# One buffer for x1*x3, four for chunks of x and f_logit, and no gate on the recurrence, in a gated recurrence followed by a Hyena convolution

## The chip, the cores and the metric

The kernel runs on one core of a Trainium2 chip. The metric is the device time of one execution in microseconds (us), the median of several executions. Profiles come from one further execution under the hardware profiler. The engines are TensorE (PE; its weight loads are shown apart as PEld), VectorE (DVE), ScalarE (ACT), GpSimd (POOL) and SyncE (SP, which here issues all DMAs). Each engine takes its instructions strictly in the order in which the program lists them for it; engines wait for each other through semaphores.

## The reference

```python
# x, f_logit: [4, 6272, 256], lower_bound: [256]
f = lower_bound + (1 - lower_bound) * sigmoid(f_logit)
h[t] = f[t] * h[t-1] + (1 - f[t]) * x[t]            # over t, h[-1] = 0
proj = h @ w_proj                                    # [4, 6272, 768]
x1, x2, x3 = split(proj, 3)                          # 256 each
x2_conv = irfft(rfft(x2, axis=1) * rfft(filter_fft, axis=0), axis=1)   # circular, length 6272
out = (x1 * x2_conv * x3) @ w_out
```

## The kernel before

The length S = 6272 is taken as 128 x 49, and the Fourier transform as two matmul stages over these factors. Before the batches, `prepare` makes the transform matrices and the spectrum of the filter, which goes to DRAM in 16 pieces `H[u]`. The first batch's recurrence runs beside it. Each batch then passes through these parts:

- `hgrn(b)`, the recurrence, in 13 chunks of 512 time steps (the last has 128). A chunk of `f_logit` and one of `x` are loaded into the buffers `FL` and `XT` (L279-282; `NX` of each, so chunk c + NX waits for the transposes of chunk c). ACT takes the sigmoid (L283), POOL multiplies with it (L285), PE transposes both (`turn`, L294; the tasks are `sT` and `uT`), ACT turns the sigmoid into f (`fTs`, L306), and DVE scans along time (L311) into the tile `HA`, whose halves hold h for the two halves of the channels. POOL copies h once more into a contiguous region of `HA` (L262, "copy E"), which phase_p reads with a stride and which also holds, as `A`, the first-stage transform (`E`) of the batch before until its unit has read it. From the second batch on, the transposes of f_logit's chunk c also wait (`late`, L288) for the inverse matmuls of unit `AFTER[c]` of the batch before.
- `phase_p(b)` (L589) projects h to x2, `phase_f1(b)` (L604) does the first transform stage, `mini(b)` the zero frequencies.
- `units(b)`: 16 units of 8 channel pairs. Each loads its piece of H into one of the `Hu` buffers (L641), does the second transform stage on PE (L648), a small copy into `PP` on POOL (L651), the product with H on DVE (L658, two of them), the inverse stage on PE (L668) and a copy of its result into `Th`.
- `gate(b, u)`, called at the end of unit u: for the row chunks in `GATES[u]`, PE computes x1 and x3 (L340, four tasks of two matmuls for one chunk), ACT copies them to `x1s` and `x3s` (L350; two buffers each), and POOL multiplies them into the tile z (L354, two per chunk). A gate of unit u > 0 waits for the second transform stage of unit u (`("F", u)`); that of unit 0 waits for the last transposes of the same batch's recurrence (`"qT"`). The gate matmuls read h in `HA`, chunks c - 1 and c, and so the next batch's scan may overwrite these chunks only behind them.
- `phase_o(b)`: the last inverse stage (L694), the product with z on DVE (L701, into `ys`), the projection by w_out (L711), a copy and the store. phase_p of the next batch waits for the stores that go out of the space behind x2.

The order of each engine's instructions is made when the program is built. Every operation is handed to `Plan.op` with a guessed cost on each engine that may do it, what it reads and what it writes; `Plan.emit` is a list scheduler. It goes through the engines, takes for each the operations that can start first by its guesses, among these the one with the longest remaining path (`level`), and issues the earliest. Costs in the code are, for n columns, 0.12 + 2.2 n/1000 us for z, 0.1 + 0.535 us per 128 time steps for the product of x and the sigmoid, 0.07 + 2.25 n/1000 for a scan. DMAs are guessed at 300 KB per us, one behind the other. All batches behind the first prepare stage are one plan, so operations of neighbouring batches may overlap as far as the listed dependences allow. PSUM's eight banks are handed out by the same planner.

z has a buffer `z0` for even batches and `z1` for odd ones, 25 KB per partition each; `z0` lies in the pool that lives from the start, `z1` in `cv`, which begins behind the first recurrence.

Of the kernel before, what the change touches and what calls it, by code (L numbers as in the profile page):

```python
# [11 lines left out]
F16 = mybir.dt.float16  # L12
# [12 lines left out]
Q = 49  # L25
TB = 98
CH = 512
NX = 2
NCHK = 13

AFTER = (2, 5, 7, 10, 12, 15)

GATES = [[0, 1, 2], [3], [4], [5], [6], [7], [8], [9], [10], [11], [12]] + [[]] * 5
XR = 10
NEP = 128
UE = 8
NU = NEP // UE
# [151 lines left out]
def kernel(  # L189
# [17 lines left out]
    konst = ctx.enter_context(tc.tile_pool(name="konst", bufs=1))  # L207
# [16 lines left out]
    HA = konst.tile([128, 2 * S + EW], F16, name="HA")  # L224
    A = HA[:, S:S + EW].rearrange("m (e r k) -> m e r k", r=2, k=64)
    HB = (0, S + EW)

    z0 = konst.tile([128, 2, Q, 128], F16, name="z0")
    XT = konst.tile([128, NX, 4, D], F32, name="XT")
    FL = konst.tile([128, NX, 4, D], F32, name="FL")  # L230
    fTs = konst.tile([128, 2, CH], F32, name="fTs")
    x1s = konst.tile([128, 2, CH], F32, name="x1s")
# [31 lines left out]
    def either(n, runs=1.0):  # L264

        return {"ACT": 0.15 + runs * n / 1200.0, "DVE": 0.15 + runs * n / 960.0}
# [4 lines left out]
    def hgrn(b):  # L271
        for c in range(NCHK):
            t0 = c * CH
            nb = min(CH, S - t0) // 128
            n = nb * 128
            k = count["x"] % NX
            count["x"] += 1
# [9 lines left out]

            late = [("U", AFTER[min(c, len(AFTER) - 1)])] if b else []  # L288
            for kh in range(2):
# [34 lines left out]


    def gate(b, u):
        z = zt[b % 2]
        for c in GATES[u]:
            m0 = c * XR
            nm = min(XR, 128 - m0)  # L330
            hn = [("hn", kh, i) for kh in range(2) for i in range(max(c - 1, 0), c + 1)]
            t0, n = m0 * Q, nm * Q
            for jb in range(2):
                x13 = []
                for i in range(2):
                    js = slice(i * 256 + jb * 128, i * 256 + jb * 128 + 128)

                    def mm(e, p, js=js, t0=t0, n=n):
                        for kh in range(2):
                            nc.tensor.matmul(PS[:, p, 0:n], W13[:, kh, js],  # L340
                                             HA[:, HB[kh] + t0:HB[kh] + t0 + n],
                                             start=(kh == 0), stop=(kh == 1))
                    x13.append(op({"PE": 2 * n / 2400.0}, mm,
                                  r=hn + ["W13", ("F", u) if u else "qT"], w=["qX"], take=1))
                j = count["s"] % 2
                count["s"] += 1
                xs = [t[:, j, 0:n] for t in (x1s, x3s)]
                for i in range(2):
                    op({"ACT": 0.15 + n / 1200.0}, lambda e, p, xs=xs[i], n=n, i=i:
                       nc.scalar.activation(  # L350
                           xs, PS[:, p, 0:n], AF.Copy, scale=1.0 if i else ZS),
                       w=[("x1s", j, i)], src=x13[i])
                op({"POOL": 0.12 + 2.2 * n / 1000}, lambda e, xs=xs,
                   zz=z[:, jb, :, m0:m0 + nm]: nc.gpsimd.tensor_tensor(  # L354
                       zz, xs[0].rearrange("p (m r) -> p r m", r=Q),
                       xs[1].rearrange("p (m r) -> p r m", r=Q), op=AOP.mult),
                   r=[("x1s", j, 0), ("x1s", j, 1)], w=[("z", b % 2, jb, c)])


    def prepare(tmp):  # L360
# [275 lines left out]
    def units(b):  # L636
        for u in range(NU):
            es = slice(u * UE, (u + 1) * UE)
            k = u % 2
            h = (b * NU + u) % 3  # L640
            op({"SP": 0.5}, lambda e, h=h, u=u: nc.sync.dma_start(Hu[:TB, h], H[u][:]),  # L641
               r=[("H", u, i) for i in range(3)], w=[("Hu", h)], kb=400)

            def mm(e, xb, es=es):
                for r in range(2):
                    for e2 in range(2):
                        rows = slice(64 * e2, 64 * e2 + 64)
                        nc.tensor.matmul(PS[:, xb + e2, :], FT[rows, r, :], A[rows, es, r, :],  # L648
                                         start=(r == 0), stop=(r == 1))
            f2 = op({"PE": 0.5}, mm, r=[("E", u)], w=[("F", u)], take=2)  # L650
            op({"POOL": 0.35}, lambda e, k=k, es=es: nc.gpsimd.tensor_copy(  # L651
                PP[:TB, k, :, :, :, 0], zm[:TB, :, :, es]), r=["zm"],
               w=[("Pz", k, 0), ("Pz", k, 1)])
            for o in range(2):
                def prod(e, xb, o=o, k=k, h=h):
                    px = PS[:TB, xb + o, :].rearrange("p (i k) -> p i k", k=64)[:, :, 1:64]
                    hh = Hu[:TB, h, :, o].rearrange("p a (i k) -> p a i k", k=64)
                    nc.vector.tensor_tensor(  # L658
                        PP[:TB, k, o, :, :, 1:64],
                        px.unsqueeze(1).broadcast_to([TB, 2, UE, 63]), hh[:, :, :, 1:64],  # L660
                        op=AOP.mult)
                op({"DVE": 1.2}, prod, r=[("Hu", h)], w=[("P", k, o)], src=f2)

            def inv(e, ib, k=k):
                for o in range(2):
                    for pr in range(UE // 2):
                        for n, v in enumerate((VA, VB)):
                            nc.tensor.matmul(PS[:, ib + o, pr * TB:(pr + 1) * TB],  # L668
                                             PP[:TB, k, o, n, 2 * pr:2 * pr + 2, :], v[:TB],
                                             start=(n == 0), stop=(n == 1))  # L670
            i2 = op({"PE": 0.96}, inv, r=[("P", k, 0), ("P", k, 1), ("Pz", k, 0), ("Pz", k, 1)],
                    w=[("U", u)], take=2)
            op(either(784), lambda e, ib, u=u: copy(
                e, Th[:, :, :, u * 4:(u + 1) * 4],
                PS[:, ib:ib + 2, 0:392].rearrange("p a (g c) -> p c a g", g=4)),
               r=[("x2", g) for g in range(13)], w=["Th", ("Th", u)], src=i2)
            gate(b, u)


    def phase_o(b):  # L680
        zr = zt[b % 2][:].rearrange("p k r m -> p k (r m)")
        tf = Th[:].rearrange("p c a g -> p (c a g)")
        for g, r0 in enumerate(range(0, Q, 4)):
            rn = min(4, Q - r0)

            def inv(e, cb, r0=r0, rn=rn):
                for i in range(rn):
# [13 lines left out]
               nc.vector.tensor_tensor(  # L701
                   y, PS[:, cb:cb + 2, 0:rn * 128], zr[:, :, r0 * 128:(r0 + rn) * 128],
                   op=AOP.mult),
               r=[("z", b % 2, jb, c) for jb in range(2) for c in range(NCHK)],
               w=[("y", yk)], src=i1)

            def proj(e, ob, y=y, rn=rn):
# [6 lines left out]
            k = count["o"] % 2  # L714
# [4 lines left out]
               r=[("x2o", i) for i in range(14)] if k else [], w=[("osb", k)], src=po)  # L719
# [3 lines left out]
               r=[("osb", k)] + ([("x2o", i) for i in range(14)] if k else []), kb=128 * rn)  # L723

    def gaps(p):

        a = X2[:, p * PW:NEP * PW].rearrange("m (i c) -> m i c", c=PW)
        nc.gpsimd.memset(a[:, :, Q:64], 0.0)
        nc.gpsimd.memset(X2[:, NEP * PW:NEP * PW + 16], 0.0)

    zt = [z0, None]
    with tc.manual_schedule():
        with tc.tile_pool(name="tmp", bufs=1) as tmp:
            prepare(tmp)
            hgrn(0)
            plan.emit()
        cv = ctx.enter_context(tc.tile_pool(name="cv", bufs=1))
        zt[1] = cv.tile([128, 2, Q, 128], F16, name="z1")
        X2 = cv.tile([128, NEP * TB + 2048], F16, name="X2")
        Th = X2[:, 0:NEP * TB].rearrange("p (c a g) -> p c a g", a=2, g=64)  # L740

        PP = cv.tile([128, 2, 2, 2, UE, 64], F16, name="PP")
        Hu = cv.tile([128, 3, 2, 2, UE * 64], F16, name="Hu")

        ys = cv.tile([128, 2, 2, 512], F32R, name="ys")
        osb = [cv.tile([128, 4, 256], F32, name="osb0"),
               X2[:, NEP * TB:NEP * TB + 2048].bitcast(F32).rearrange("p (r e) -> p r e", e=256)]
        zm = cv.tile([128, 2, 2, NEP], F16, name="zm")
        gaps(0)
        phase_p(0)  # L750
        phase_f1(0)
        mini(0)
        for b in range(B):
            units(b)
            phase_o(b)
            if b + 1 < B:
                hgrn(b + 1)
                phase_p(b + 1)
                phase_f1(b + 1)
                mini(b + 1)  # L760
        plan.emit()
# [30 lines left out]
```

## Time and profile before

| | us |
|---|---|
| median of 3 runs | 607.95 (606.51 to 609.89) |
| the profiled execution | 613.48 |
| its span, first to last instruction | 611.7 |
| mean granted TensorE clock | 0.917 |

| part | first to last instruction of the line, us |
|---|---|
| scans of the four batches (L311) | 20.2-100.3, 150.2-237.2, 290.0-372.8, 420.4-505.2 |
| phase_p (L589) | 102.7-113.9, 237.7-248.6, 373.8-384.6, 505.5-516.4 |
| second transform stage of the units (L648) | 125.6-183.9, 260.2-312.4, 396.3-452.4, 528.1-570.0 |
| z (L354) | 102.4-190.7, 237.7-321.0, 373.6-458.5, 505.7-577.1 |
| projection in phase_o (L711) | 193.5-234.0, 322.3-362.6, 461.8-502.0, 578.6-604.6 |

A busy time is the time in which an engine worked on an instruction; the share is of the span or of the stretch. A row of the table by stretches gives the stretch, its length, the busy time of each engine with the number of instructions in brackets, the clock granted to TensorE (1.00 is full), the mean share of the 16 DMA engines and what they moved in GB/s. For a single line the same row holds that line's instructions only. A row of a timeline gives start, duration, engine, line, operation, the tiles written and read, the shape and the count; an idle time of the engine before it stands in brackets, with the instruction that ended it. `SPq` is SP's sequencer, whose rows are the issues of DMAs. A row of the waits gives who waited for whom, the total in us, how often, and the longest.

### The profile page before, as it was taken

How to read it: one execution, taken by the hardware profiler on the slowest of the kernel's cores; microseconds unless marked ns; L12 is line 12 of the kernel's file. 1: busy time of each engine (PE TensorE's matmuls, PEld its weight loads, DVE VectorE, ACT ScalarE, POOL GpSimd, SP SyncE). 2: the span in 40 equal slices, each digit the busy share in tenths (PEclk: the TensorE clock that was granted, in tenths of full speed). 3: DMA queues.
4: the chain of work that ended last, by engine and by line, in shares of the span. 5: the costliest groups of instructions: out<-in, count | busy, mean ns of one | idle time of the engine just before them, and what ended most of it. 6: DMA issues, size and time to landing. Idle time of an engine off the chain costs nothing. (4 is left out here: it accounts for less than half of the span.)

```text
span 611.7 us, 12552 instructions
## 1 busy us (share of the span) xinstructions
PE 505.6 (83%) x4821; PEld 377.6 (62%) x4821; DVE 470.2 (77%) x450; ACT 409.6 (67%) x568; POOL 396.0 (65%) x362
## 2 busy tenths in 40 slices
PE   1679977979889888979897859979887969799793
PEld 1668755846457777836466848736466858455483
DVE  8966863899958676989859756899868857989661
ACT  4787774957666577948675656958675759668443
POOL 4455556647998558649896557557995653669700
PEclk9987996979989898979989988989989989989886
DMA  9975888115847897025848984027658960135055
GB/s 313 337 251 193 288 287 259 50 55 177 225 122 230 291 349 244 1 80 158 251 147 283 318 315 139 1 88 226 204 155 266 359 245 11 28 130 168 21 207 215
DMA packets 73038, 117.57 MB, mean 192 GB/s; under 512 B 4366, under 2 KB 55634, under 8 KB 72978
## 3 DMA queue, kind: packets, MB, share of 16 engines
q1 hardware_dynamic: 72978, 116.77, 57.5%
q8 instruction: 38, 0.62, 0.4%
q14 instruction: 22, 0.18, 0.1%
HBM read 84.54 MB, written 32.11 MB: 191 GB/s over the span
## 5 line engine op out<-in xcount | busy, mean ns | idle before, releaser
L354 POOL TENSOR_TENSOR z<-x1s,x3s 128x490 f16<-128x490 f32 (+1 forms) x104 | 200.1, 1938 | 61.7 <-ACT x3s L350 58.8
L658 DVE TENSOR_TENSOR PP<-PS,Hu 98x1008 f16<-98x1008 f32 x128 | 146.3, 1199 | 26.1 <-PE PS L648 7.9
L311 DVE TENSOR_TENSOR_SCAN HA<-fTs,HA,PS 128x512 f16<-128x512 f32 (+1 forms) x96 | 114.7, 1206 | 47.6 <-PE PS L294 38.2
L285 POOL TENSOR_TENSOR XT<-XT,FL 128x1024 f32<-128x1024 f32 (+1 forms) x52 | 118.0, 2271 | 42.7 <-DMA XT<-in_x_dram 22.5
L340 PE MATMUL PS<-HA,W 128*128 128x490 f16 (+1 forms) x416 | 111.3, 388 | 4.1 <-ACT x1s L350 3.3
L252 ACT CAST X<-PS 128x784 f16<-128x784 f32 (+2 forms) x82 | 82.4, 1013 | 32.4 <-PE PS L668 27.3
L294 PE MATMUL PS<-iden,XT 128*128 128x128 f32 x392 | 70.8, 306 | 35.5 <-POOL XT L285 31.5
L262 POOL COPY HA<-HA 128x512 f16<-128x512 f16 (+3 forms) x100 | 59.0, 598 | 61.6 <-DVE HA L311 59.1
L306 ACT ACTIVATE fTs<-PS,nomc 128x512 f32<-128x512 f32 (+1 forms) x104 | 68.7, 664 | 42.2 <-PE PS L294 36.2
L350 ACT ACTIVATE x1s<-PS 128x490 f32<-128x490 f32 (+1 forms) x104 | 60.4, 581 | 43.3 <-PE PS L340 22.1
L294 PE MATMUL PS<-iden,FL 128*128 128x128 f32 x392 | 67.6, 297 | 20.9 <-ACT FL L283 18.6
L294 PEld LDWEIGHTS PS<-iden,XT 128*128 128x128 f32 x392 | 49.2, 155 | 51.1 <-POOL XT L285 36.5
L668 PEld LDWEIGHTS <-PP 98*128 98x128 f16 x1024 | 57.0, 105 | 31.7 <-POOL PP L651 19.1
L701 DVE TENSOR_TENSOR ys<-PS,z 128x1024 fp32r<-128x1024 f32 (+1 forms) x52 | 59.3, 1154 | 19.1 <-PE PS L694 13.8
L668 PE MATMUL PS<-VA,PP 98*128 98x98 f16 x512 | 58.3, 219 | 16.8 <-POOL PP L651 16.0
L340 PEld LDWEIGHTS <-W 128*128 128x128 f16 x416 | 37.3, 102 | 54.1 <-issue 35.1
L711 PE MATMUL PS<-Wo,ys 128*128 128x256 f32 x392 | 63.5, 308 | 5.9 <-DVE ys L701 3.8
L283 ACT ACTIVATE FL<-FL 128x1024 f32<-128x1024 f32 (+1 forms) x52 | 52.4, 1010 | 23.0 <-DMA FL<-in_f_logit_dram 23.0
L294 PEld LDWEIGHTS PS<-iden,FL 128*128 128x128 f32 x392 | 50.3, 153 | 27.8 <-issue 15.5
L350 ACT ACTIVATE x3s<-PS 128x490 f32<-128x490 f32 (+1 forms) x104 | 59.6, 573 | 5.3 <-PE PS L340 5.0
L257 DVE CAST X<-PS 128x1024 f16<-128x1024 f32 (+2 forms) x34 | 45.7, 1369 | 19.4 <-PE PS L589 9.7
L711 PEld LDWEIGHTS PS<-Wo,ys 128*128 128x128 f32 x392 | 53.7, 204 | 9.8 <-issue 3.4
(91 smaller groups left out, 657.4 us busy)
## 6 DMA issues: line engine op xcount, KB each, us to landing
Hu<-H SPq DMA_DIRECT2D x64, 392.0 KB
FL<-in_f_logit_dram SPq DMA_DIRECT2D x48, 512.0 KB
XT<-in_x_dram SPq DMA_DIRECT2D x48, 512.0 KB
out_dram<-X SPq DMA_DIRECT2D x24, 512.0 KB
out_dram<-osb SPq DMA_DIRECT2D x24, 512.0 KB
HA<-in_moe_filter_fft_dram SPq DMA_DIRECT2D x12, 512.0 KB
H<-HA SPq DMA_DIRECT2D x16, 196.0 KB
H<-HA SPq DMA_DIRECT2D x32, 98.0 KB
```

The lines of the kernel that those rows point to most:

```text
L252: nc.scalar.copy(dst, src)
L285: op({"POOL": 0.1 + 0.535 * nb}, lambda e, xt=xt, ft=ft: nc.gpsimd.tensor_tensor(xt, xt, ft, op=AOP.mult), r=[("ft", k)], w=[("xt", k)])
L294: nc.tensor.transpose(PS[:, p, j * 128:(j + 1) * 128], src[:, j, cols], iden[:])
L306: nc.scalar.activation(fT, PS[:, p, 0:n], AF.Identity, scale=nomc[:, kh:kh + 1], bias=1.0),
L311: nc.vector.tensor_tensor_scan(h, fT, PS[:, p, 0:n], init, op0=AOP.mult, op1=AOP.add),
L340: nc.tensor.matmul(PS[:, p, 0:n], W13[:, kh, js], HA[:, HB[kh] + t0:HB[kh] + t0 + n], start=(kh == 0), stop=(kh == 1))
L350: nc.scalar.activation(xs, PS[:, p, 0:n], AF.Copy, scale=1.0 if i else ZS),
L354: zz=z[:, jb, :, m0:m0 + nm]: nc.gpsimd.tensor_tensor(zz, xs[0].rearrange("p (m r) -> p r m", r=Q), xs[1].rearrange("p (m r) -> p r m", r= ...
L658: nc.vector.tensor_tensor(PP[:TB, k, o, :, :, 1:64], px.unsqueeze(1).broadcast_to([TB, 2, UE, 63]), hh[:, :, :, 1:64], op=AOP.mult)
L668: nc.tensor.matmul(PS[:, ib + o, pr * TB:(pr + 1) * TB], PP[:TB, k, o, n, 2 * pr:2 * pr + 2, :], v[:TB], start=(n == 0), stop=(n == 1))
L701: nc.vector.tensor_tensor(y, PS[:, cb:cb + 2, 0:rn * 128], zr[:, :, r0 * 128:(r0 + rn) * 128], op=AOP.mult),
L711: nc.tensor.matmul(po[:, i, :], y[:, kh, i * 128:(i + 1) * 128], Wo[:, kh, :], start=(kh == 0), stop=(kh == 1))
```

## The change

Only z's single tile `zt` remains, allocated in `cv`; the keys of its parts lose the batch's number, so z of a batch waits for the readers of the batch before. `NX` goes from 2 to 4, the `Hu` buffers from 3 to 4. `AFTER` becomes `(0,)`: every chunk of the next recurrence waits for unit 0 alone. `GATES` puts chunks 0 to 2 at unit 0 as before and two chunks at each of units 1 to 5, instead of one at each of units 1 to 10.

```diff
-NX = 2
+NX = 4
-AFTER = (2, 5, 7, 10, 12, 15)
-
-GATES = [[0, 1, 2], [3], [4], [5], [6], [7], [8], [9], [10], [11], [12]] + [[]] * 5
+AFTER = (0,)
+
+GATES = [[0, 1, 2], [3, 4], [5, 6], [7, 8], [9, 10], [11, 12]] + [[]] * 10
@@ the kernel's tiles
-
-    z0 = konst.tile([128, 2, Q, 128], F16, name="z0")
@@ gate
-        z = zt[b % 2]
+        z = zt
-                   r=[("x1s", j, 0), ("x1s", j, 1)], w=[("z", b % 2, jb, c)])
+                   r=[("x1s", j, 0), ("x1s", j, 1)], w=[("z", jb, c)])
@@ units
-            h = (b * NU + u) % 3
+            h = (b * NU + u) % 4
@@ phase_o
-        zr = zt[b % 2][:].rearrange("p k r m -> p k (r m)")
+        zr = zt[:].rearrange("p k r m -> p k (r m)")
-               r=[("z", b % 2, jb, c) for jb in range(2) for c in range(NCHK)],
+               r=[("z", jb, c) for jb in range(2) for c in range(NCHK)],
@@ the end of the kernel
-    zt = [z0, None]
-        zt[1] = cv.tile([128, 2, Q, 128], F16, name="z1")
+        zt = cv.tile([128, 2, Q, 128], F16, name="zt")
-        Hu = cv.tile([128, 3, 2, 2, UE * 64], F16, name="Hu")
+        Hu = cv.tile([128, 4, 2, 2, UE * 64], F16, name="Hu")
```

## The prediction, made before the changed kernel was run

> **What bounds the kernel now.** First the page: its head, the engines' busy time (share of the span) and three groups. Then the table by stretches, whose borders are the starts and ends of the stages in the timeline.
>
> ```profile
> span 611.7 us, 12552 instructions
> PE 505.6 (83%) x4821; PEld 377.6 (62%) x4821; DVE 470.2 (77%) x450; ACT 409.6 (67%) x568; POOL 396.0 (65%) x362
> L306 ACT ACTIVATE fTs<-PS,nomc 128x512 f32<-128x512 f32 (+1 forms) x104 | 68.7, 664 | 42.2 <-PE PS L294 36.2
> L283 ACT ACTIVATE FL<-FL 128x1024 f32<-128x1024 f32 (+1 forms) x52 | 52.4, 1010 | 23.0 <-DMA FL<-in_f_logit_dram 23.0
> FL<-in_f_logit_dram SPq DMA_DIRECT2D x48, 512.0 KB
> ```
>
> ```profile
> core 0: us, PE busy (x) PEld busy (x) DVE busy (x) ACT busy (x) POOL busy (x), PEclk, DMA share, GB/s
> 125.60:190.00 64.40, 54.12 (x483) 32.37 (x484) 53.18 (x48) 40.55 (x67) 50.65 (x45) 0.89 0.55 162
> 190.00:237.70 47.70, 39.36 (x423) 33.79 (x424) 35.30 (x32) 29.75 (x40) 28.99 (x30) 0.93 0.86 292
> 237.70:260.20 22.50, 22.18 (x243) 19.50 (x242) 18.74 (x15) 21.23 (x25) 16.60 (x8) 1.00 0.21 67
> 260.20:318.20 58.00, 51.41 (x468) 30.75 (x468) 48.13 (x43) 39.31 (x66) 46.40 (x42) 0.88 0.49 152
> 318.20:373.80 55.60, 42.00 (x440) 36.24 (x440) 39.58 (x35) 31.95 (x43) 33.55 (x34) 0.91 0.82 285
> 396.30:457.70 61.40, 52.04 (x482) 31.46 (x480) 53.12 (x48) 40.59 (x67) 50.62 (x45) 0.94 0.55 163
> 457.70:505.50 47.80, 38.32 (x422) 33.14 (x423) 35.30 (x32) 30.02 (x40) 29.08 (x30) 0.96 0.84 285
> 528.10:575.40 47.30, 41.34 (x407) 22.29 (x408) 42.00 (x38) 32.76 (x56) 39.14 (x35) 0.93 0.36 112
> 575.40:604.60 29.20, 24.74 (x294) 21.27 (x294) 15.03 (x13) 10.25 (x10) 1.75 (x2) 0.84 0.42 169
> ```
>
> No engine is full over the span. A batch has three stages: phase_p and phase_f1 (22.5 us, PE busy for 22.18: full); the units (64.4, 58.0, 61.4, and 47.3 in the last batch, where no recurrence runs beside them); and phase_o with the rest of the next batch's recurrence (47.7, 55.6, 47.8; alone 29.2 to its last projection). **The pair "units and phase_o" takes 112.1, 113.6 and 109.2 us, mean 111.6. There the change works, three times.** In the phase_o stage no engine is full and the DMAs stand at 0.82 to 0.86. What ends last there is the round trip of a chunk of x; rows from the timelines of SP, ACT, POOL and PE (start, duration, in brackets the idle time before and its releaser):
>
> ```profile
> 326.16 0.37 SPq L280 DMA_DIRECT2D FL<-in_f_logit_dram  x1
> 330.96 1.05 ACT L283 ACTIVATE FL<-FL 128x1024 f32<-128x1024 f32 x1
> 334.39 2.35 POOL L285 TENSOR_TENSOR XT<-XT,FL 128x1024 f32<-128x1024 f32 x1
> 336.80 0.66 PE L294 MATMUL PS<-iden,XT 128*128 128x128 f32 x4 [1.96 <-POOL XT L285]
> 337.96 0.37 SPq L280 DMA_DIRECT2D FL<-in_f_logit_dram  x1
> 367.63 1.11 PE L294 MATMUL PS<-iden,XT 128*128 128x128 f32 x4 [3.98 <-POOL XT L285]
> ```
>
> Load, sigmoid, product, transposes; only then may the same buffer be loaded again: 337.96 - 326.16 = 11.8 us for two chunks, 5.9 each. PE stands and waits for the product, 1.96 us here and 3.98 later.
>
> **The change, part by part.** *NX 2 to 4.* Four buffers allow a chunk every 11.8 / 4 = 3.0 us; then the round trip no longer decides, and the engines are late next. Two more chunks are loaded and multiplied in the phase_p stage, where the DMAs stand at 0.21 and POOL has 22.5 - 16.6 = 5.9 us free for 2 x 2.35 = 4.7. I price that at nothing; without this room the first z's slip by 4.7.
>
> *AFTER = (0,).* Every chunk may be transposed from unit 0 on, so work moves from phase_o into the units; how much, the planner decides. The table by stretches for single lines, first the transposes (L294):
>
> ```profile
> 125.60:190.00 64.40, 12.64 (x76) 9.30 (x76) 0.89 0.55 162
> 260.20:318.20 58.00, 9.01 (x60) 7.37 (x60) 0.88 0.49 152
> 318.20:373.80 55.60, 21.54 (x137) 17.34 (x136) 0.91 0.82 285
> 396.30:457.70 61.40, 12.09 (x76) 9.00 (x76) 0.94 0.55 163
> ```
>
> Then z (L354), the copies of PP (L651) and the copies of h (L262):
>
> ```profile
> 260.20:318.20 58.00, 36.02 (x19) 0.88 0.49 152
> 260.20:318.20 58.00, 4.91 (x16) 0.88 0.49 152
> 318.20:373.80 55.60, 11.89 (x20) 0.91 0.82 285
> ```
>
> And all engines in three pieces of the second units stage:
>
> ```profile
> 260.20:270.00 9.80, 5.93 (x42) 2.46 (x40) 9.21 (x9) 3.55 (x6) 4.58 (x5) 0.86 0.13 43
> 280.00:320.00 40.00, 37.14 (x372) 24.03 (x369) 32.11 (x28) 30.65 (x52) 37.32 (x35) 0.91 0.63 191
> 300.00:310.00 10.00, 7.53 (x56) 3.93 (x54) 5.53 (x6) 5.40 (x9) 10.00 (x10) 0.74 0.59 186
> ```
>
> A chunk is 16 transposes, so the units hold 76/16, 60/16 and 76/16 = 4.75, 3.75, 4.75 chunks, mean 4.4. After the change? In the planner the units' operations have the longer remaining path, so the recurrence fills gaps; and its scan of chunk c waits for the gate matmuls of chunk c + 1. I take 7, with 5 and 13 as the bounds. What goes with the 2.6 chunks more: on ACT a sigmoid and two fTs, 1.0 + 2 x 0.66 = 2.3 us each, 6 us where 58.0 - 39.3 are free; two loads of 512 KB, about 2.7 MB beside the 152 GB/s x 58 us = 8.8 MB now, at a DMA share of 0.49. Neither decides. POOL does, it is the queue in which the copies of PP stand behind products and z's, and the units' inverse matmuls wait for those copies.
>
> Units with 7 chunks, by POOL: z 36.0, PP 4.9, four products that weren't made ahead x 2.35 = 9.4, 12 copies of h x 0.6 (11.89 / 20) = 7.2; together 57.5. The first 9.8 us hold 4.6 as now; the other 52.9 at the share that POOL reaches from 280 to 320 (37.3 of 40, 93%) take 57: **66.7**. By a straight line instead: the mean stage of 61.3 less 47.3 is 14.0 for 4.4 chunks, 3.2 each, and 2.6 more give 69.6. I take 68.
>
> The phase_o stage with the other 6, by PE: 24.7 alone, and per chunk 16 x 21.54 / 137 = 2.5; more closely packed 2.2 (my estimate: four transposes of 0.66 overlap at their ends). 24.7 + 13.2 = 37.9, at 93% **40.8**, against 50.4 in the mean now. Pair: 108.8 - 111.6 = -2.8, **three times -8**. A further chunk in the units costs (2.35 + 1.2) / 0.93 = 3.8 there and saves 2.2 / 0.93 = 2.4 behind, net 1.4: from 9 chunks on nothing is left of the gain.
>
> PEclk is 0.84 where phase_o runs alone and 1.00 in the full phase_p stage; after the gap of 3.98 us four transposes took 1.11 instead of 0.66. The Trainium skill, "TensorE: Matmul & The Clock Gate", section "HAM oscillation", says that PE gaps above about 3.4 us throttle the clock again; the trace agrees. By that rule a phase_o without such gaps runs at full clock, and the sum would be lower by about 4 a pair, 12 in all; the sum here leaves that out.
>
> *GATES in pairs.* Only a permission. It helps where POOL is idle early in the units; POOL in the last batch, and DVE's wait for Hu there:
>
> ```profile
> 537.14 0.33 POOL L651 COPY PP<-zm 98x32 f16<-98x32 f16 x1 [1.53 <-PE PS L668]
> 540.46 1.95 POOL L354 TENSOR_TENSOR z<-x1s,x3s 128x490 f16<-128x490 f32 x1 [3.00 <-ACT x3s L350]
> DVE PP L658 <- DMA Hu<-H: 0.8, 1, 0.8
> ```
>
> Behind 540 z's and PP copies follow almost without a gap, so z is behind its permission already. In the last batch the idle 3.0 may go to z: -2 (from -4 to +3, where two z's of 1.95 are put ahead of a PP copy). The planner counts a z as 0.12 + 2.2 x 0.49 = 1.2 us, the row says 1.95: what POOL does there comes later than planned.
>
> *One z.* A new wait: z of batch b + 1 behind the last ys of phase_o(b). DVE and POOL:
>
> ```profile
> 357.04 0.40 DVE L701 TENSOR_TENSOR ys<-PS,z 128x256 fp32r<-128x256 f32 x1
> 373.64 4.09 POOL L354 TENSOR_TENSOR z<-x1s,x3s 128x490 f16<-128x490 f32 x2 [0.47 <-ACT x3s L350]
> ```
>
> The reader is 16 us earlier; with a recurrence that ends 10 us sooner it still is: nothing. If not, z holds up the h copies and products behind it on POOL, and through x1s and x3s ACT, by the lateness itself, up to 5 us.
>
> *Four Hu.* One wait of 0.8 us is all that DVE spends on Hu in the last batch: nothing, from -1 to +1 (SP's loads of H go earlier and so do the loads of x behind them).
>
> *The prepare stage.* SP's loads of chunks 7 and 11, and two stretches:
>
> ```profile
> 54.42 0.40 SPq L280 DMA_DIRECT2D FL<-in_f_logit_dram  x1
> 85.08 0.40 SPq L280 DMA_DIRECT2D FL<-in_f_logit_dram  x1
> 50.00:75.00 25.00, 24.97 (x186) 19.68 (x185) 19.60 (x17) 19.10 (x23) 13.66 (x21) 0.95 0.82 275
> 75.00:100.70 25.70, 17.81 (x115) 12.90 (x113) 14.48 (x14) 14.71 (x20) 13.53 (x18) 0.85 0.78 270
> ```
>
> A chunk takes (85.08 - 54.42) / 4 = 7.7 us. Up to 75 PE is full; behind it nothing is, and four buffers may save up to 25.7 - 17.8 = 8. Against that the DMAs stand at 0.8, and two more chunks at the front push the filter's loads back by 2 MB, some 7 us. I take -4, from -8 to +5.
>
> **Sum:** -8 - 4 - 2 = -14. The profiled execution took 613.5 us (611.7 of span, 1.8 around it), so 599.5; the median shown, 608.0, is 5.5 below, and I carry the difference over: **594**.
>
> **Rivals.** *POOL holds the units: slower.* The planner, with its cheap z, lets nearly all chunks into the units, and PP copies queue behind products. It decides from 9 chunks on; with 13 a pair costs -2.8 + 6 x 1.4 = +5.6, three times +17, less 6 for prepare and last batch: **619**. For it: from 300 to 320 POOL has hardly a gap, and in the first half of that DVE falls to 5.5 of 10. Against it: the units' longer paths. *The round trip was all.* POOL runs the units without a gap, 9.8 + 52.9 = 62.7, and PE runs phase_o at full clock, (24.7 x 0.84 + 13.2) / 0.93 = 36.5: 99.2, three times -12.4, with -8 in prepare and -2: **561**. For it: PE's waits from 357 to 368; against it: POOL's 93%. *The permission isn't used.* z keeps its pace of one per unit, the scans wait for the gates, and the recurrence enters as slowly as now; the tails alone shrink, by 1 us each: **605**.
>
> **How the numbers follow.** Forecast 0.47, slower rival 0.22, round trip 0.15, unused permission 0.16. A measurement of this kernel can tell about 0.5%, 3 us, from no change. Faster: 0.42 + 0.15 + 0.05 = 0.62; same: 0.04 + 0.08 + 0.02 = 0.14; slower 0.24. The range runs to the outer rivals, 566 to 621: with bad ends of prepare and last batch the slower one passes it, and the round trip's own price lies outside.
>
> **What would show it.** The forecast: units of 66 to 70 us with about 112 transposes in them, phase_o near 41, no wait of PE for L285 of 2 us or more, under 8 us from the last ys to phase_p. It is wrong if the units pass 75 or phase_o stays at 48. The price of one z is wrong if L354 waits for L701, that of Hu if L658 waits for DMA in more than one place, that of prepare if phase_p(0) doesn't start before 100.

## The result, and the profile after

The changed kernel takes 585.4 us (median of 4, 578.5 to 592.4) against 608.9 for the kernel before (median of 4, 606.5 to 610.7). Executions of the changed kernel fall into two groups, 577 to 581 and 590 to 595 us, and the ratio, 0.951 with a 95% interval of 0.946 to 0.957, is that of the faster ones, as are all ratios below. Forecast were 594 and a range of 566 to 621: the direction and the range hold, the gain was 23.5 us by the medians and 30 by the ratio where 14 were forecast, and it did not come the way the forecast said.

The head of the page after, and its row for the DVE copies of phase_p (L255, before L257):

```profile
span 590.6 us, 12576 instructions
PE 505.9 (86%) x4821; PEld 375.7 (64%) x4821; DVE 458.7 (78%) x442; ACT 413.2 (70%) x577; POOL 391.7 (66%) x362
L255 DVE CAST X<-PS 128x1024 f16<-128x1024 f32 (+2 forms) x27 | 38.7, 1450 | 33.5 <-DMA out_dram<-X 24.1
```

The table by stretches of the kernel after, borders as in the prediction: prepare, then phase_p with phase_f1, units and phase_o of each batch in turn; the last two rows are the last batch's units and the end.

```profile
0.00:116.40 116.40, 87.13 (x449) 68.06 (x449) 77.19 (x109) 65.16 (x83) 51.19 (x71) 0.77 0.70 230
116.40:143.60 27.20, 22.86 (x242) 19.58 (x242) 19.51 (x16) 21.92 (x28) 18.88 (x12) 1.00 0.74 222
143.60:194.10 50.50, 45.95 (x458) 26.88 (x456) 45.75 (x43) 38.77 (x65) 47.92 (x41) 1.00 0.53 152
194.10:242.50 48.40, 42.57 (x455) 36.48 (x455) 40.60 (x37) 32.90 (x45) 34.35 (x33) 0.96 0.95 322
242.50:271.40 28.90, 23.09 (x237) 19.84 (x237) 16.25 (x13) 22.94 (x27) 18.04 (x12) 0.94 0.26 91
271.40:317.40 46.00, 43.58 (x443) 25.13 (x444) 43.85 (x40) 35.69 (x61) 41.33 (x38) 1.00 0.47 143
317.40:372.60 55.20, 46.40 (x480) 37.22 (x480) 40.57 (x37) 40.38 (x56) 43.62 (x38) 0.99 1.01 347
372.60:396.80 24.20, 22.04 (x228) 19.57 (x229) 15.79 (x13) 19.96 (x21) 10.10 (x7) 0.87 0.02 6
396.80:442.90 46.10, 43.76 (x430) 24.62 (x430) 42.31 (x38) 34.92 (x60) 40.52 (x37) 0.96 0.48 142
442.90:489.90 47.00, 42.98 (x476) 37.20 (x475) 42.25 (x38) 34.50 (x48) 33.09 (x33) 1.00 0.91 322
489.90:513.00 23.10, 22.46 (x245) 19.52 (x245) 19.25 (x16) 20.30 (x25) 12.51 (x9) 1.00 0.01 2
513.00:556.50 43.50, 39.53 (x407) 21.31 (x407) 40.34 (x37) 33.09 (x57) 40.16 (x36) 1.00 0.38 113
556.50:590.60 34.10, 23.59 (x294) 20.25 (x294) 15.03 (x13) 12.68 (x13) 0.00 (x0) 0.80 0.47 189
```

| stage | before, us | after, us |
|---|---|---|
| prepare | 102.7 | 116.4 |
| phase_p and phase_f1, four batches | 22.9, 22.5, 22.5, 22.6 | 27.2, 28.9, 24.2, 23.1 |
| units | 64.4, 58.0, 61.4, 47.3 | 50.5, 46.0, 46.1, 43.5 |
| phase_o, the last with the end | 47.7, 55.6, 47.8, 36.3 | 48.4, 55.2, 47.0, 34.1 |

So the units lost 45 us, phase_o kept its length, and prepare (+14) and phase_p (+13) gave 27 back. That is the 21 us between the two spans. In the profiled execution (592.4 us), and in the one profiled again in e1 (592.3), PE ran a part of the prepare stage at half clock:

```profile
60.00:80.00 20.00, 20.00 (x90) 15.29 (x90) 11.07 (x10) 10.18 (x12) 12.54 (x14) 0.53 0.36 111
80.00:100.00 20.00, 20.00 (x83) 14.61 (x82) 7.99 (x7) 7.02 (x8) 3.79 (x11) 0.50 0.43 132
```

PE is busy in all of these 40 us and its clock (the third column from the right) is 0.53 and 0.50; it waits for nothing there, and the DMAs are at 0.36 and 0.43. The profiles of e3, e4, e7, e10 and e12, whose prepare stage is the same as the changed kernel's, have a clock of 0.74 to 0.83 from 60 to 80 us and 1.00 from 80 to 100, and phase_p starts at 100.3 to 103.8. So the 14 us belong to the execution and not to the order of the instructions.

**The recurrence went the other way.** The transposes (L292 after the change) in the three units stages that have a next recurrence:

```profile
143.60:194.10 50.50, 7.21 (x52) 5.68 (x52) 1.00 0.53 152
271.40:317.40 46.00, 4.46 (x36) 3.89 (x36) 1.00 0.47 143
396.80:442.90 46.10, 2.93 (x24) 2.59 (x24) 0.96 0.48 142
```

That is 3.25, 2.25 and 1.5 chunks where the kernel before had 4.75, 3.75 and 4.75 and the forecast had 7. Ungated, the recurrence kept out of the units. The remaining 9, 10 and 10.75 chunks then pass beside phase_o in the 47 to 55 us that 7.5 or 8.5 took before. What the round trip cost PE shows in the page's row for the transposes, before (x's, L294) and after (L292):

```profile
L294 PE MATMUL PS<-iden,XT 128*128 128x128 f32 x392 | 70.8, 306 | 35.5 <-POOL XT L285 31.5
```

```profile
L292 PE MATMUL PS<-iden,XT 128*128 128x128 f32 x392 | 65.6, 290 | 11.8 <-POOL XT L283 5.0
```

The idle time that the product of x and the sigmoid ended went from 31.5 to 5.0 us.

**A new wait in phase_p.** Two answers of the waits, for the stretches 242.5 to 271.4 and 372.6 to 396.8, then DVE's and SP's timelines at the first:

```profile
DVE X L255 <- DMA out_dram<-X: 9.6, 1, 9.6
DVE X L255 <- DMA out_dram<-X: 14.6, 1, 14.6
```

```profile
238.44 1.77 SPq L278 DMA_DIRECT2D FL<-in_f_logit_dram  x1
240.30 1.50 SPq L278 DMA_DIRECT2D XT<-in_x_dram  x1
241.89 1.95 SPq L718 DMA_DIRECT2D out_dram<-X  x1
250.84 2.78 DVE L255 CAST X<-PS 128x1024 f16<-128x1024 f32 x2 [9.59 <-DMA out_dram<-X]
```

phase_p may write x2 only when the last store out of that space has landed. This store is issued at 241.89, behind the eight loads of the next recurrence's first four chunks, which four buffers let in early, and lands 9 us later; DVE stands for 9.6 us. The wait of 14.6 us costs less than it shows: it begins ahead of the stage, PE starts that phase_p at 372.58 only, and the stretch is 24.2 us long against 22.5 before.

### The profile page after: what moved, and what is told of

Its sections match the earlier page's. It is cut to its first block, busy times and chain, and to the rows that moved or that the text cites. A ratio compares the mean times of both kernels' runs of the same rounds, so it can differ in the third digit from the quotient of the medians.

```text
span 590.6 us, 12576 instructions
## 1 busy us (share of the span) xinstructions
PE 505.9 (86%) x4821; PEld 375.7 (64%) x4821; DVE 458.7 (78%) x442; ACT 413.2 (70%) x577; POOL 391.7 (66%) x362
## 4 chain that ended last, share of the span: by engine, by line
PE 36%; DMA 12%; ACT 8%; DVE 7%; POOL 6%; issue 3%; SPq 0%; ACTq 0%; DVEq 0%
PE PS L338 8%; DMA out_dram<-X 7%; PE PS L666 6%; PE PS L292 6%; POOL zt L352 5%; PE PS L646 5%; PE PS L587 4%; PE PS L709 4%; DMA FL<-in_f_logit_dram 3%; DVE HA L309 2%; ACT X L250 2%; DVE HA L255 2%; PE PS L692 2%; ACT X L252 2%; PE PS L602 1%
## 5 line engine op out<-in xcount | busy, mean ns | idle before, releaser
L352 POOL TENSOR_TENSOR zt<-x1s,x3s 128x490 f16<-128x490 f32 (+1 forms) x104 | 203.8, 1980 | 48.1 <-ACT x3s L348 47.5
L338 PE MATMUL PS<-HA,W 128*128 128x490 f16 (+1 forms) x416 | 101.4, 369 | 5.1 <-ACT X L250 2.7
L250 ACT CAST X<-PS 128x784 f16<-128x784 f32 (+2 forms) x89 | 88.1, 1002 | 12.4 <-PE PS L587 5.5
L292 PE MATMUL PS<-iden,XT 128*128 128x128 f32 x392 | 65.6, 290 | 11.8 <-POOL XT L283 5.0
L292 PE MATMUL PS<-iden,FL 128*128 128x128 f32 x392 | 65.2, 290 | 7.7 <-ACT FL L281 4.0
L699 DVE TENSOR_TENSOR ys<-PS,zt 128x1024 fp32r<-128x1024 f32 (+1 forms) x52 | 58.8, 1151 | 15.6 <-PE PS L692 11.7
L666 PEld LDWEIGHTS <-PP 98*128 98x128 f16 x1024 | 51.2, 98 | 21.2 <-POOL PP L649 7.2
L255 DVE CAST X<-PS 128x1024 f16<-128x1024 f32 (+2 forms) x27 | 38.7, 1450 | 33.5 <-DMA out_dram<-X 24.1
L292 PEld LDWEIGHTS PS<-iden,XT 128*128 128x128 f32 x392 | 46.6, 147 | 19.6 <-POOL XT L283 6.2
L666 PE MATMUL PS<-VA,PP 98*128 98x98 f16 x512 | 52.8, 208 | 6.3 <-POOL PP L649 3.4
L587 PE MATMUL PS<-W,HA 128*128 128x256 f16 x392 | 50.1, 289 | 9.0 <-ACT X L250 3.9
```

Of the source, the lines that this page charges most:

```text
L250: nc.scalar.copy(dst, src)
L292: nc.tensor.transpose(PS[:, p, j * 128:(j + 1) * 128], src[:, j, cols], iden[:])
L338: nc.tensor.matmul(PS[:, p, 0:n], W13[:, kh, js], HA[:, HB[kh] + t0:HB[kh] + t0 + n], start=(kh == 0), stop=(kh == 1))
L352: zz=z[:, jb, :, m0:m0 + nm]: nc.gpsimd.tensor_tensor(zz, xs[0].rearrange("p (m r) -> p r m", r=Q), xs[1].rearrange("p (m r) -> p r m", r= ...
L587: nc.tensor.matmul(pp[:, r - r0, :], HA[:, n0:n0 + Q * 127 + 1:Q], W2[:, kh, :], start=(kh == 0), stop=(kh == 1))
L666: nc.tensor.matmul(PS[:, ib + o, pr * TB:(pr + 1) * TB], PP[:TB, k, o, n, 2 * pr:2 * pr + 2, :], v[:TB], start=(n == 0), stop=(n == 1))
```

## The experiments

The runs of the kernel before, on the same chips, had medians of 608.9 to 609.3.

| run | median, us | ratio to before, 95% interval |
|---|---|---|
| e1 changed kernel again | 584.9 | 0.947 (0.940 to 0.954) |
| e2 two buffers for x | 590.1 | 0.963 (0.955 to 0.971) |
| e3 recurrence lifted into the units | 614.2 | 1.007 (1.003 to 1.011) |
| e4 held until unit 15 | 580.1 | 0.952 (0.947 to 0.957) |
| e5 before, gates in pairs | 610.3 | 1.003 (0.999 to 1.007) |
| e6 before, one z, ungated | 608.2 | 0.999 (0.995 to 1.002) |
| e7 single gates | 591.0 | not given |
| e8 prepare on two buffers | 578.5 | 0.946 (0.937 to 0.955) |
| e9 two buffers for x, three for H | 606.9 | 0.996 (0.993 to 1.000) |
| e10 late loads | 562.9 | 0.922 (0.917 to 0.927) |
| e11 late loads, prepare on two, output buffers anew | 560.0 | 0.918 (0.914 to 0.922) |
| e12 three H buffers | 591.6 | 0.972 (0.961 to 0.983) |

**e1, the changed kernel again.**

> The changed kernel itself, as the measure for the others and for a second profile. Its profile showed the prepare stage 14 us longer than before, with PE at half clock from 60 to 100 us. Theory A (the half clock belongs to that one execution): here the prepare stage ends near 100 to 105 and the whole takes 577 to 582. Theory B (it belongs to the change, because the filter's work starts 16 us later): the prepare stage again ends near 115 and the whole takes about 590.

Its runs were 592.3, 577.3, 577.5 and 595.1. Neither theory alone: in the profile taken here the half clock is back and phase_p starts at 118.4, but two executions took 577, and e4 and e10, with the same prepare stage, have full clock from 80 us on in their profiles. That it is in about half the executions is concluded from their times; only two were profiled.

**e2, two buffers for x and f_logit.**

```diff
-NX = 4
+NX = 2
```

> Changed kernel, but two buffers for x and f_logit. Theory R (the gain is the round trip of a chunk: four buffers let the recurrence run beside phase_o at about 3.5 us a chunk instead of 5.7): the pair of units and phase_o goes back to 108 to 113 us, the time to 600 to 612. Rival U (ungating, gates in pairs and the fourth H buffer gave it): 580 to 588, pairs near 98.

590.1, between the two. The pairs of units and phase_o are 105.9, 108.7 and 106.4, at or a little below R's figure, against 98.9, 101.2 and 93.1 in the changed kernel; but prepare is 100.7 and phase_p's stretches are 22.8 to 23.4. The four buffers win some 28 us in the pairs and lose most of it around them (16 of that in prepare, at the half clock). The round trip is back, as PE's waits for the product in the whole kernel show, 33.6 us against 5.0:

```profile
PE PS L292 <- POOL XT L283: 33.6, 25, 3.8
```

And with two buffers 19 us of gain remain, which round trips don't explain; e5, e6 and e9 look for them.

**e3, the recurrence lifted into the units.** The planner's remaining path of its operations grows by 40, and nothing else changes:

```diff
+        for i in todo:
+            ops[i]["level"] += ops[i]["lift"]
...
+                plan.lift = 40.0
                 hgrn(b + 1)
+                plan.lift = 0.0
```

> Changed kernel, but the planner adds 40 us to the remaining path of the next recurrence's operations, so that 45 to 52 of its 52 transposes are issued ahead of the last unit's inverse matmuls, where the changed kernel issues 3 to 9. Theory K (the changed kernel is faster because the recurrence keeps out of the units): units of 75 to 90 us, phase_o near 35, pairs 110 to 120, the time 605 to 640. My recorded sum puts the pair at 108.8 with seven chunks and 1.4 more for each further one, so 115 to 117 for all thirteen: about 620. Rival (with four buffers it doesn't matter where the recurrence runs): pairs 95 to 101, 575 to 590.

614.2. The first pair, units and phase_o, by stretches:

```profile
131.10:214.20 83.10, 68.09 (x602) 46.54 (x601) 68.70 (x61) 58.80 (x94) 75.07 (x70) 0.91 0.72 212
214.20:245.90 31.70, 29.17 (x319) 22.56 (x320) 19.37 (x18) 14.66 (x21) 14.46 (x10) 0.90 0.66 239
```

Units of 83.1, with POOL busy for 75.1 of them (90%), and a phase_o of 31.7: the pairs are 114.8, 111.5 and 111.8, some 15 us above the changed kernel's. Theory K's figures hold, and the sum of the slower rival (117 for 13 chunks) is 2 to 6 above. The order alone is worth 29 us by the medians and 34 by the ratios.

**e4, the recurrence held until unit 15.**

```diff
-AFTER = (0,)
+AFTER = (15,)
```

> Changed kernel, but every chunk of the next recurrence waits for unit 15, so none is in the units. Theory K (the recurrence keeps out of the units anyway, ungating is a permission that is hardly used): within 1% of the changed kernel, 573 to 587. Rival (the one or two chunks that do enter the units give the gain): 590 to 600.

580.1, ratio 0.952 as the changed kernel. The first pair:

```profile
128.60:175.80 47.20, 42.66 (x418) 23.44 (x416) 40.77 (x38) 34.63 (x59) 44.74 (x38) 0.96 0.45 133
175.80:231.00 55.20, 47.93 (x497) 40.21 (x496) 46.07 (x41) 37.87 (x53) 38.30 (x37) 0.97 0.97 332
```

Units of 47.2 with POOL at 95%, and a phase_o of 55.2, nearly the whole recurrence in it, at a DMA share of 0.97. In the time, ungating brings nothing that a full gate wouldn't; in the profiles the pairs are 11.5 us longer in sum than the changed kernel's (102.3, 103.9, 98.5), and prepare and the stretches of phase_p are shorter.

**e5, the kernel before with gates in pairs.**

```diff
-GATES = [[0, 1, 2], [3], [4], [5], [6], [7], [8], [9], [10], [11], [12]] + [[]] * 5
+GATES = [[0, 1, 2], [3, 4], [5, 6], [7, 8], [9, 10], [11, 12]] + [[]] * 10
```

> The kernel before with GATES in pairs and nothing else changed. Theory G (early z's are the larger half of the gain, because they fill POOL while it stood idle early in every batch's units): the units get 4 to 7 us shorter in each batch, the last from 47.3 to about 43.5; the time 588 to 596. Rival (the gain of the run with two buffers came from the ungated recurrence or the fourth H buffer): within 0.7% of before, 604 to 612. My recorded price for this edit was -2 us in all: 606.

610.3: theory G falls, for this kernel. The first units stage and the last:

```profile
125.00:188.20 63.20, 52.39 (x481) 30.86 (x481) 51.04 (x45) 40.98 (x69) 49.97 (x45) 0.95 0.56 169
528.80:573.40 44.60, 39.46 (x406) 21.29 (x405) 41.09 (x37) 33.08 (x57) 39.63 (x36) 1.00 0.40 119
```

The last units, without a recurrence, take 44.6 instead of 47.3; those with one stay as they were.

**e6, the kernel before with one z and AFTER = (0,).**

> The kernel before with one z and AFTER = (0,), two buffers for x and the old GATES. The planner puts every engine's instructions in the same order as before; only the semaphores differ. Theory G: within 0.5% of before, 605 to 612. Rival (z's single buffer makes phase_p's z wait, or ungating lets transposes go early): 612 to 620 or below 600.

608.2, as theory G had it: one z and ungating together change nothing. The three units stages hold 76, 60 and 76 transposes, as before the change, so the permission alone isn't used.

**e7, the changed kernel with single gates.** The edit of e5 undone in the kernel after.

> The changed kernel with the old GATES, one chunk at a unit. Theory G: the units get 4 to 6 us longer in each batch, the time 590 to 602. Rival (with the recurrence out of the units z has room anyway): 575 to 586.

591.0 (580.7 to 598.4), 6 above the changed kernel, with a spread that is wider than that. In its profile the last units take 47.6 against 43.5, but the pairs 94.4, 101.4 and 94.7 are no longer than the changed kernel's. So the gates in pairs gain in the last batch, some 4 us in these profiles, of which 2.5 are PE's busy time (42.0 against 39.5) at a clock of 0.93 against 1.00; beyond it this run is inconclusive.

**e8, the first recurrence on two buffers.**

```diff
-            k = count["x"] % NX
+            k = count["x"] % (NX if b else 2)
```

> The changed kernel, but the first batch's recurrence uses two of the four buffers, so that the prepare stage is planned as before. Theory P (four buffers bring x ahead of the filter's loads, the filter's matmuls come late and in one block, and PE may stay at half clock there): phase_p starts at 100 to 104 in every execution, the median is 574 to 580 with all runs within 1%, against 585 with runs from 577 to 595. Rival (the half clock is a matter of the execution alone): single runs of 588 to 595 remain.

578.5, with runs from 573.6 to 585.1: no 590, but not within 1% either. From 60 to 80 us PE has its full clock, and phase_p starts at 102.1:

```profile
60.00:80.00 20.00, 18.13 (x135) 13.43 (x134) 14.47 (x12) 14.33 (x17) 12.13 (x18) 1.00 0.83 273
222.10:254.10 32.00, 24.04 (x237) 20.19 (x237) 15.79 (x13) 24.28 (x27) 17.62 (x12) 0.89 0.18 62
```

The second row is phase_p with phase_f1 of the second batch: 32.0 us, PE busy in 24.0 of them. The new wait is still there, 8.1 us of it. Five profiles with four buffers in the prepare stage have full clock from 80 us on too, so this run can't decide for theory P.

**e9, two buffers for x and three for H.** e2 with `% 4` for Hu turned back to `% 3`.

> The changed kernel with two buffers for x and f_logit and three for H; it differs from the kernel before by the pairs in GATES, AFTER and one z only. Pairs alone gave 610 and one z with the ungated recurrence 608, all three with four H buffers 590. Theory H (the fourth H buffer is what gave that, with or without the others): 604 to 612. Rival I (pairs and ungating need each other: early gate matmuls release h early, and only an ungated recurrence can use it): 588 to 596.

606.9: theory H. Together with e2 the fourth H buffer is worth 17 us where x has two. The recurrence's place doesn't explain it: the units hold 188 transposes in both. POOL's order does in part. At the start of the first units stage POOL makes three z's ahead of the first copies of PP in e9, and two in e2 (the first two rows). PE's waits for these copies in the whole kernel are 15.8 us in e9 and 4.5 in e2 (the last two), and the four units stages are 18 us shorter in e2:

```profile
130.10 5.87 POOL L352 TENSOR_TENSOR zt<-x1s,x3s 128x490 f16<-128x490 f32 x3 [2.99 <-ACT x3s L348]
127.01 4.00 POOL L352 TENSOR_TENSOR zt<-x1s,x3s 128x490 f16<-128x490 f32 x2 [3.00 <-ACT x3s L348]
PE PS L666 <- POOL PP L649: 15.8, 5, 3.4
PE PS L666 <- POOL PP L649: 4.5, 3, 1.5
```

**e10, late loads.**

```diff
-                   w=[t], kb=n)
+                   r=[("F", 0)] if b and c in (2, 3) else [], w=[t], kb=n)
-                ft, ft, AF.Sigmoid, scale=-1.0), r=["sin"], w=[("ft", k)], table="sigmoid")
+                ft, ft, AF.Sigmoid, scale=-1.0), r=["sin"] + ([("U", 13)] if b and c in (2, 3) else []), w=[("ft", k)], table="sigmoid")
```

> The changed kernel, but of the next recurrence's chunks 2 and 3 the loads wait for unit 0 of the batch that runs, and their sigmoids for unit 13. In the changed kernel's profile phase_p and phase_f1 take 28.9 and 24.2 us instead of 22.5, DVE waiting 9.6 and 14.6 us there for the last store out of the space of x2, which shares the DMA queues with four chunks' loads. Theory D (these loads delay that store): that wait falls under 3 us, phase_p and phase_f1 are back at 22 to 24 us, the time 570 to 578 where the prepare stage runs at full clock. Rival (the store is late because the recurrence ends early; the wait turns into another): stretches of 25 us and more, 577 to 590.

562.9, better than theory D hoped for. DVE's wait in phase_p of the second batch, and then phase_p with phase_f1 of the second batch, units, phase_o, and phase_p with phase_f1 of the third:

```profile
DVE X L255 <- DMA out_dram<-X: 2.9, 1, 2.9
```

```profile
222.40:246.30 23.90, 22.63 (x243) 19.73 (x241) 17.51 (x14) 22.82 (x29) 16.81 (x10) 1.00 0.35 113
246.00:289.00 43.00, 40.63 (x421) 22.50 (x419) 39.61 (x37) 34.19 (x59) 39.28 (x35) 1.00 0.48 143
289.00:345.00 56.00, 48.86 (x499) 40.73 (x498) 47.18 (x43) 38.76 (x52) 43.04 (x39) 0.97 0.88 308
345.00:369.00 24.00, 22.53 (x245) 19.50 (x245) 18.35 (x16) 20.89 (x23) 12.98 (x10) 1.00 0.32 105
```

9.6 became 2.9, the stretch 23.9, and PE is busy in 22.6 of it. phase_p with phase_f1 of the first batch is 29.5, no shorter than the changed kernel's 27.2; with two buffers in the prepare stage it is 24.1 (e8) and 23.6 (e11). By the ratios late loads are worth 15 to 18 us, by the medians 22. But prepare apart, this profile is 14 us shorter than the changed kernel's, and only 5 of them lie in the four stretches of phase_p; about 10 lie in the units, which hold 20, 16 and 20 transposes instead of 52, 36 and 24. The edit holds two sigmoids back as well as the loads, so it doesn't show what the store alone is worth.

**e11, the three together.** e8 and e10, and in phase_o `k = g % 2` in place of the running count.

> As the run with late loads, with the first batch's recurrence on two buffers, and with the output buffers of phase_o starting anew in each batch, so that the last full store before a phase_p always leaves from the separate buffer. Theory D with theory P: 562 to 572, no run above 580. Rival: no better than the two alone, 574 to 580.

560.0 (556.7 to 566.5), a little below the theory's range, 0.918 of before and the fastest here; 3 us better than e10, which the spread of the two just covers.

**e12, three H buffers in the changed kernel.**

> The changed kernel with three H buffers instead of four, four for x and f_logit. With two for x the fourth H buffer was worth 17 us (607 against 590) without DVE ever waiting 2 us for an H load. Theory L (it works through the planner's order, by taking the units' path below or beside the recurrence's; with four buffers for x the recurrence's path is already the shorter one, so it adds nothing): within 1.2% of the changed kernel, 578 to 592. Theory W (H loads are really waited for behind loads of x on SP's queue): 595 to 605.

591.6 (585.3 to 598.1), the upper end of L; but the ratio of 0.972 lies above those of e1 and of the first runs, and the intervals don't meet. So the fourth H buffer is worth 6 us here by the medians and 13 to 15 by the ratios, less than in e9, and L's "nothing" doesn't hold. DVE's waits for H, in e9 (where the longest, 3.1, is above the 2 us of the expectation) and here:

```profile
DVE PP L656 <- DMA Hu<-H: 5.5, 4, 3.1
DVE PP L656 <- DMA Hu<-H: 0.4, 1, 0.4
```

In e9 such waits are 5.5 of the 17 us, here 0.4, so theory W falls. PE's waits for the copies of PP are 15.2 us here against 3.4 in the changed kernel, nearly the difference between e9 and e2. So a good part of the fourth buffer's worth lies in the order that the planner makes (e7, with four H buffers and single gates, has 13.9, so it takes the gates in pairs too); that a shorter path for the units brings this order is argued, not shown.

## Why the prediction was right or wrong

**What bounds the kernel** held: the work of the change is in the pairs, and beside phase_o the round trip of a chunk ended last. The stage took 47.7 / 7.5 = 6.4 us a chunk before and 47.0 / 10.75 = 4.4 to 55.2 / 10 = 5.5 after, phase_o's own work included. Where I had the engines as late next, the DMAs are nearly full: a share of 0.91 to 1.01 in the three phase_o stages after, up from 0.82 to 0.86. That they end last there isn't shown; e10's second phase_o is as long at 0.88.

**The number came in by luck, in part.** The three pairs won 41.7 us where 8 were forecast, and prepare and the stretches of phase_p gave 27 back where 4 were to be won. By its own signs the prediction of the pairs was wrong: units of 46 to 51 us instead of 66 to 70, phase_o still at 47 to 55 instead of 41.

**The step that failed is "I take 7".** The prediction said itself that the units' operations have the longer remaining path and that the recurrence fills gaps; it then let more chunks into the units because the gate was gone. But part of the recurrence's remaining path ran through its buffers, load behind load. With four of them that chain has half as many rounds, so its path shortened, and the planner put it behind the units' work almost everywhere: 1.5 to 3.25 chunks. Worked out from the costs in the code, and not measured: the path from a recurrence's first transposes to the next phase_p is 57 us with two buffers and 33.5 with four, and from a unit's second transform stage 43 for the last unit and 64 or more for the first; with two buffers the first chunks are ahead of the last units, with four none is ahead of any. The runs agree; transposes in the three units stages, by buffers:

| | three for H | four for H |
|---|---|---|
| two for x | 68, 52, 68 (e9) | 60, 52, 76 (e2) |
| four for x | 20, 24, 24 (e12) | 52, 36, 24 (changed) |

e3 shows that it is the path that decides (40 added, all else alike, and all chunks go in), e6 that the gate did not: there the third rival's "the permission isn't used" was right.

**The sum for a pair** was nearly right about what it priced. With the recurrence in the units e3's pairs came to 111.5 to 114.8 where the sum gives 117. It read the sign rightly too, a further chunk in the units costs more than it saves; the case of fewer chunks, which follows from the same line, was left out: 2.3 chunks instead of 7 give 108.8 - 4.7 x 1.4 = 102.2, and 97.7 was the mean. Pairs of -13, -12 and -16 were the result, where -2.8 each was forecast.

**NX 2 to 4 "at nothing" in phase_p** was mis-sized. POOL had the room; the stores didn't. The four chunks' loads delay the last store, and phase_p with phase_f1 lose 13 us over the four batches, 6.4 of them in the second, where the wait is, and 1.7 in the third. The first batch's 4.3 can't be that, no store precedes it; they are nearly gone with two buffers in the prepare stage (24.1 in e8, 23.6 in e11). e10 takes two of the chunks' loads away and has the second batch's stretch back at 23.9. The prediction counted the bytes of the loads, not whose turn they took.

**Gates in pairs**, -2 in the last batch: e5 has 2.7, but that doesn't show the price. e9's last units have the same gates and H buffers and take 47.1. In both PE waits 3.44 us for the first copies of PP; here is what followed, e5 and then e9:

```profile
538.00 0.22 PE L668 MATMUL PS<-VA,PP 98*128 98x98 f16 x1 [3.44 <-POOL PP L651]
538.00:543.00 5.00, 5.00 (x64) 3.12 (x64) 3.63 (x5) 3.27 (x6) 3.01 (x5) 1.00 0.35 92
543.40 0.26 PE L666 MATMUL PS<-VA,PP 98*128 98x98 f16 x1 [3.44 <-POOL PP L649]
543.40:548.40 5.00, 5.00 (x41) 2.94 (x42) 2.56 (x4) 1.62 (x2) 2.48 (x4) 0.50 0.28 82
```

The clock stays full in e5 and is halved in e9, and PE's busy time in the stage differs by the 2.5 us that lie between the two (39.46 and 41.95). In the changed kernel, with the fourth H buffer, this wait is 1.5 us and the clock stays full: 43.5.

The price of **one z**, nothing: e6. **Four Hu** at -1 to +1 was wrong: 17 us in e9 against e2, and 6 to 15 in e12. I read the waits for H of before, 0.8 us in the last batch, but the buffer also changes POOL's order, and PE waits for that.

**Prepare**, -4: 100.3 to 103.8 in five profiles, so -2 to +1; at half clock +14 and +16, inside no bound that I gave. By the prediction's sign (phase_p not before 100) this price was wrong too.

**The clock.** The rule of the Trainium skill that the prediction cites would have phase_o's clock rise once PE waits less: 0.93, 0.91, 0.96 became 0.96, 0.99, 1.00, and the units' 0.89, 0.88, 0.94 became 1.00, 1.00, 0.96. PE's busy time in the three units stages fell from 157.6 to 133.3 us, fewer transposes included; how much of that is clock is not separated.

## What to carry to other kernels

Where a list scheduler orders the work, a buffer is also a priority: count what an added buffer does to the remaining paths, and ask which of two pieces of work will now give way, before pricing overlap. A buffer that lets loads go early sends them ahead of somebody's stores; look for the store that opens the next stage, and hold the loads until the DMAs have room (here, with the sigmoids held too, 15 us or more beside the change's own 23.5). And where a stage's first instructions differ between two orders, look there for a wait of PE, and at the clock behind it.

## What the runs showed of the hardware that I had not expected

PE stayed at a granted clock of 0.50 to 0.53 for 40 us in which it was busy without a gap (the rows from 60 to 100 us), in both profiled executions of one program; e4 and e10, with the same prepare stage, had 0.83 from 60 to 80 and 1.00 from 80 to 100. The Trainium skill, "TensorE: Matmul & The Clock Gate", section "Seeing it yourself", reports that the clock gate has been seen stuck, at a quarter and for over 50 us; here it was a half. What sets it off isn't settled by these runs.

The same wait of PE, 3.44 us behind the same work, was followed by full clock in e5 and by half clock for 5 us in e9.

The DMAs moved 347 GB/s over the 55.2 us of the second phase_o stage, at a share of 1.01, against 285 and 0.82 before.
